# HGRN2 attention with a bilinear feed-forward: the first two units get output tiles, a queue and state sums of their own

## The chip, the core and the metric

The kernel runs on one core of a Trainium2 chip. The metric is the device time of one execution in microseconds (us). The kernel before took 626.97 us (median of 3 runs, 625.71 to 627.32). The engines of the core are TensorE (PE, with its weight load PEld), VectorE (DVE), ScalarE (ACT), GpSimd (POOL) and SyncE (SP). Each works through its own list of instructions in order, and they wait for each other by semaphores.

## The reference, cut to what matters

The first half is a gated linear attention, the second a feed-forward block without an activation function. The output of the first is the input of the second.

```python
# q, k, v, f_logit: (4, 8, 768, 48) = batch, heads, sequence, head_dim
f = 1.0 / (1.0 + np.exp(-f_logit))
for t in range(S):
    state = f[:, :, t, :, None] * state + np.einsum('bhd,bhe->bhde', k[:, :, t], v[:, :, t])
    y[:, :, t] = np.einsum('bhd,bhde->bhe', q[:, :, t], state)

# x: (3072, 384) = the y of all heads side by side; w_a, w_b: (384, 1536); w_out: (1536, 384)
out = (x @ w_a) * (x @ w_b) @ w_out
```

The three weights arrive as 64-bit floats and are turned into 32-bit ones on the chip.

## The kernel before

The attention is cut into 16 units. A unit is one batch, one half of the sequence (384 tokens) and four heads. The feed-forward of a block of 384 tokens needs two units (`NQ` is 2), so the first block can start when units 0 and 1 have delivered their y. The names of the stages:

- `front(u)`: sigmoid of the gates (ACT), running products by scans (DVE), q and k multiplied with them (DVE).
- `scores(u)`: k times q in blocks of 64 tokens (PE), then a causal mask (DVE).
- `turn(u)`: k transposed on PE, copied to `kT` by ACT.
- `within(u)`: v times the masked scores (PE, into `ps_y` or two banks of `ps_f`).
- `gains(u)`: what each sub-block of 64 tokens adds to the state (PE, into `ps_x`), then the states at the sub-blocks' borders, summed one after the other on DVE:

```python
        for n in range(2):
            for c in range(NC):
                for p in range(2):
                    ...
                    for h in range(2):
                        r = slice(SUB * p, SUB * p + SUB)
                        nc.tensor.matmul(
                            ps_x[R * h:R * h + D, p, (n * NC + c) * D:(n * NC + c) * D + D],
                            lhsT=kT[r, n, c, R * h:R * h + D],
                            rhs=t["v"][r, n, c, h * D:h * D + D],
                            start=True,
                            stop=True,
                        )
        ...
        for j in range(NJ - 1 if last else NJ):
            c, p = divmod(j, 2)
            new = ps_x[:, p, 0:2 * NC * D].rearrange("r (n c d) -> r n c d", n=2, c=NC)[:, :, c]
            if before is None:
                nc.vector.tensor_copy(st[:, j], new)
            else:
                nc.vector.tensor_tensor(st[:, j], before, new, ALU.add)
            before = st[:, j]
        before = live[u]["st"][-1]
        if not last:

            for n in range(2):
                end = products_of_f[u][:, n, BLK - 1:BLK]
                nc.vector.tensor_scalar(before[:, n], before[:, n], end, math.exp(-MIDDLE), ALU.mult, ALU.mult)
```

- `across(u)`: the states times q (PE, added to what `within` left), then y copied out of PSUM and sent by DMA into `xT`, the input of the feed-forward with channels on partitions:

```python
        y = sb1.tile([128, 2 * NC, 2, SUB], FP32, tag="y", name="y")

        whole = [(0, 0, 0, 128)] if ps[0] is y_banks[0] else [(0, 0, 0, D), (0, R, R, D)]
        for p, e, r, rows in (*whole, (1, R, 0, D), (1, 0, R, D)):
            copy = nc.vector.tensor_copy if u in FIRST and p else nc.scalar.copy
            copy(y[r:r + rows, :, p], ps[p][e:e + rows, 0:BLK].rearrange("r (o m) -> r o m", m=SUB))
        give_back(ps)
        ...
        for n in range(2):
            for h in range(2):
                ...
                    queue = nc.scalar if u < NQ and (n + h) % 2 else nc.sync
                    queue.dma_start(out=xT[blk][p:p + w, kt], in_=y[row:row + w, n])
```

The pool `sb1` has one buffer for each tag, so all units share one y tile. Each unit sends its y in five transfers.

- `load_weights()` starts the load of one piece of the weights (SP). `begin(n)` and `end(n)` turn piece n into 32-bit floats: four ACT instructions and one of POOL in `begin`, two of DVE in `end`. Piece 0 and 1 are the first 128 columns of w_b and w_a, pieces 2 and 3 the next 256 columns of each.
- `up(blk, ft)`: one 128-column tile of `x @ w_b` and of `x @ w_a` on PE, 384 tokens wide, three `kt` steps each; `product()` multiplies the two.

The order in which all this is issued is written out by hand for the beginning. In the kernel before, from unit 0's last steps to the first feed-forward tile:

```python
        within(0)
        gains(0)
        load_unit(NSET, "f")
        load_weights()
        next(fronts[2])
        turn(1, True)
        across(0)
        load_weights()
        scores(1, True)
        end(2)
        within(1, True)
        load_unit(2, "q")
        gains(1)
        across(1)
        load_weights()
        next(fronts[2])
        next(fronts[3])
        end(3)
        next(fronts[2])
        up(0, 0)
```

After this beginning a loop issues the rest: the feed-forward with the remaining attention units in between.

Of the kernel before, what the change touches and what calls it, by code (L numbers as in the profile page):

```python
# [25 lines left out]
R = 64  # L26
# [52 lines left out]
def by_quotients(ctx, tc, q, k, f_logit, v, moe_w_a, moe_w_b, moe_w_out, out, ident, weights, bad):  # L79
# [171 lines left out]
    def halves(x):  # L251
        return x.rearrange("p n s -> p (n s)")

    def front(u):

        t = sets[u % NSET]
        x = halves(t["f"])
        F = halves(products_of_f[u])
        inv = invs[u % 2 if u < 2 * NQ else 0]
        if u in FIRST:  # L260
            nc.scalar.activation(F, x, AF.Sigmoid)
        nc.scalar.activation(inv, x, AF.Sigmoid, bias=less, scale=-1.0, accum_out=tails[:, u:u + 1])  # L262
        if u not in FIRST:
            nc.scalar.activation(x, x, AF.Sigmoid)

        nc.gpsimd.tensor_scalar(inv, inv, EXP_K, 1.0, ALU.mult, ALU.add)  # L266
        yield
        none = zero.broadcast_to((128, BLK))
        for n in range(2):
            c = slice(n * BLK, n * BLK + BLK)  # L270
            nc.vector.tensor_tensor_scan(F[:, c], F[:, c], none, math.exp(MIDDLE), ALU.mult, ALU.add)
        nc.vector.tensor_tensor(held[:, u], products_of_f[u][:, :, BLK - 1], least, ALU.is_ge)
        yield

        start = sb2.tile([128, 2, NC - 1], FP32, tag="start", name="start")
        nc.vector.reciprocal(start, products_of_f[u].rearrange("p n (c m) -> p n c m", m=C)[:, :, 0:NC - 1, C - 1])
        for n in range(2):
            for c in range(NC):
                w = slice(n * BLK + c * C, n * BLK + c * C + C)
                first = start[:, n, c - 1:c] if c else math.exp(-MIDDLE)  # L280
                nc.vector.tensor_tensor_scan(inv[:, w], inv[:, w], none[:, 0:C], first, ALU.mult, ALU.add)
        yield
        nc.vector.tensor_tensor(halves(t["q"]), halves(t["q"]), F, ALU.mult)
        nc.vector.tensor_tensor(halves(t["k"]), halves(t["k"]), inv, ALU.mult)
        live[u] = {}
        yield
# [68 lines left out]
    def gains(u):  # L355

        _, half, _ = unit(u)
        t, kT = sets[u % NSET], live[u]["kT"]
        last = half == NH - 1
        for n in range(2):  # L360
            for c in range(NC):
                for p in range(2):
                    if last and c == NC - 1 and p == 1:
                        continue
                    for h in range(2):
                        r = slice(SUB * p, SUB * p + SUB)
                        nc.tensor.matmul(  # L367
                            ps_x[R * h:R * h + D, p, (n * NC + c) * D:(n * NC + c) * D + D],
                            lhsT=kT[r, n, c, R * h:R * h + D],
                            rhs=t["v"][r, n, c, h * D:h * D + D],  # L370
                            start=True,
                            stop=True,
                        )
        st = sb3.tile([128, NJ, 2, D], FP32, tag="st", name="st")
        before = live[u - NQ]["st"][NJ] if half else None
        live[u]["st"] = [before] + [st[:, j] for j in range(NJ - 1 if last else NJ)]
        for j in range(NJ - 1 if last else NJ):
            c, p = divmod(j, 2)
            new = ps_x[:, p, 0:2 * NC * D].rearrange("r (n c d) -> r n c d", n=2, c=NC)[:, :, c]
            if before is None:  # L380
                nc.vector.tensor_copy(st[:, j], new)
            else:
                nc.vector.tensor_tensor(st[:, j], before, new, ALU.add)
            before = st[:, j]
        before = live[u]["st"][-1]
        if not last:

            for n in range(2):
                end = products_of_f[u][:, n, BLK - 1:BLK]
                nc.vector.tensor_scalar(before[:, n], before[:, n], end, math.exp(-MIDDLE), ALU.mult, ALU.mult)  # L390
# [19 lines left out]
    def across(u):  # L410

        b, half, qd = unit(u)
        qf, st, ps = halves(sets[u % NSET]["q"]), live[u]["st"], live[u]["y"]

        for n, c, o in reversed(list(each())) if half else each():
            for p in range(2):
                j = 2 * c + p
                if j == half == 0:
                    continue
                for h in range(2):  # L420
                    r, e = slice(R * h, R * h + D), R * (p ^ h)
                    nc.tensor.matmul(  # L422
                        ps[p][e:e + D, o:o + SUB],
                        lhsT=st[j][r, n],
                        rhs=qf[r, tokens(n, c, p)],
                        start=False,
                        stop=True,
                        skip_group_check=True,
                    )
        y = sb1.tile([128, 2 * NC, 2, SUB], FP32, tag="y", name="y")  # L430

        whole = [(0, 0, 0, 128)] if ps[0] is y_banks[0] else [(0, 0, 0, D), (0, R, R, D)]
        for p, e, r, rows in (*whole, (1, R, 0, D), (1, 0, R, D)):
            copy = nc.vector.tensor_copy if u in FIRST and p else nc.scalar.copy
            copy(y[r:r + rows, :, p], ps[p][e:e + rows, 0:BLK].rearrange("r (o m) -> r o m", m=SUB))  # L435
        give_back(ps)
        y = y.rearrange("r (n c) p m -> r n (c p m)", n=2)

        blk = b * NH + half
        if qd == 0:  # L440
            xT[blk] = sb2.tile([128, NKT, BLK], FP32, tag="xT", name="xT")
        for n in range(2):
            for h in range(2):
                ch, row, left = (4 * qd + 2 * n + h) * D, R * h, D
                while left:
                    kt, p = divmod(ch, 128)
                    w = min(left, 128 - p)

                    queue = nc.scalar if u < NQ and (n + h) % 2 else nc.sync
                    queue.dma_start(out=xT[blk][p:p + w, kt], in_=y[row:row + w, n])  # L450
                    ch, row, left = ch + w, row + w, left - w
        live.pop(u - NQ, None)
        if u >= NQ:
            load_unit(u + NSET)
# [246 lines left out]
    with tc.manual_schedule():  # L701
# [11 lines left out]

        load_unit(0, "f")
        load_unit(1, "f")
        next(fronts[0])
        load_unit(1, "q")
        load_unit(0, "q")
        load_unit(1, "k")
        load_weights()  # L720
        load_unit(0, "k")
        load_weights()
        patterns()
        next(fronts[0])
        load_weights()
        next(fronts[0])
        load_unit(1, "v")
        next(fronts[1])
        next(fronts[1])
        next(fronts[0])  # L730
        load_unit(0, "v")
        next(fronts[1])
        begin(3)
        load_unit(2, "k")
        load_unit(2, "f")
        scores(0)
        load_unit(2, "v")
        next(fronts[1])
        turn(0, True)
        within(0)  # L740
        gains(0)
        load_unit(NSET, "f")
        load_weights()
        next(fronts[2])
        turn(1, True)
        across(0)
        load_weights()
        scores(1, True)
        end(2)
        within(1, True)  # L750
        load_unit(2, "q")
        gains(1)
        across(1)
        load_weights()
        next(fronts[2])
        next(fronts[3])
        end(3)
        next(fronts[2])


        up(0, 0)
        next(fronts[2])
        load_unit(NSET, "q")
        begin(4.5)
        load_weights()
        product()
        load_unit(NSET, "v")
        end(4)
        scores(2, True)
        up(0, 1)  # L770
        next(fronts[3])
        load_unit(NSET + 1, "q")
        end(5)
        load_unit(NSET, "k")
        end(6)
        within(2)
        load_unit(NSET + 1, "f")
        load_unit(NSET + 1, "k")
        turn(2, True)
        load_weights()  # L780
        gains(2)
        load_unit(NSET + 1, "v")
        next(fronts[3])
        next(fronts[3])
        product()
        begin(7)
        up(0, 2)
        product()
        across(2)
        up(0, 3)  # L790
        begin(8)
        scores(3)
        turn(3, True)
        within(3)
        gains(3)
        across(3)
        up(0, 4)
        end(7)
        product()
        product()  # L800
        end(8)

# [446 lines left out]
```

## Time and profile before

| what | before |
| --- | --- |
| time, median of 3 runs | 626.97 us |
| span of the profiled execution | 624.1 us |
| PE busy | 588.6 us (94%) |
| DVE busy | 377.8 us (61%) |
| ACT busy | 221.6 us (36%) |
| POOL busy | 63.0 us (10%) |
| PE's share of the chain that ended last | 89% |

The busy times are sums over the whole span. What matters for one stage is read from that stage: the table by windows gives, for a stretch of time, the busy time of each engine, the clock that was granted to TensorE (1.00 is full speed) and the share of the 16 DMA engines that was busy. The view of waits says which instruction's end ended an idle time. The chain follows the last instruction back to whatever released it. In these views L435 is the copy of y out of PSUM, L450 the transfer of y into xT, L469 the feed-forward's matmuls in `up`, L216 the last step of the weights' conversion, L367 the matmuls of `gains`, L381 and L383 the states on DVE, and L188 the load of a piece of the weights. fp32 matmuls appear twice in the counts: `gains` has 24 matmuls and x48 in the trace, `up` 6 and x12. "ACTq" and "SPq" are the queues' own instructions, such as issuing a transfer.

### The profile page before, as it was taken

To read this page: it belongs to the slowest core of one execution; us is meant where nothing else is said; L and a number is where in the kernel's file an instruction comes from. 1 tells how busy PE (TensorE), PEld (TensorE's weight loads), DVE (VectorE), ACT (ScalarE), POOL (GpSimd) and SP (SyncE) were. 2 spreads that over 40 slices of the span, in tenths; PEclk is the share of its full clock that TensorE was granted. 3 is DMA by queue.
4 is the path that set the end of the run, shared out by engine and by line. 5 is a ranking of instruction groups with operands and counts; after the bars stand their busy time and mean duration, and the time that the engine had idled before them with its cause. 6 is when DMAs were issued, how large, how long until landed. Compare 5 with 4: busy or idle time off the path is not lost.

```text
span 624.1 us, 13969 instructions
## 1 busy us (share of the span) xinstructions
PE 588.6 (94%) x5922; PEld 534.5 (86%) x5922; DVE 377.8 (61%) x748; ACT 221.6 (36%) x400; POOL 63.0 (10%) x58
## 2 busy tenths in 40 slices
PE   0759899999999999999999999999999999999995
PEld 0626555558998999999999999999999999999995
DVE  6777445797877567746676476756665244534541
ACT  5578499822332243224312332233311232022200
POOL 6334154410000000000000000000000000000000
PEclk9969999999999999999999999999999999999998
DMA  8886875000045404040404003050001000000000
GB/s 215 230 274 188 181 254 193 1 1 1 32 121 114 100 2 96 6 118 1 97 1 120 28 14 85 1 122 2 21 0 46 26 8 13 2 27 0 1 26 30
DMA packets 30343, 43.65 MB, mean 70 GB/s; under 512 B 3776, under 2 KB 24896, under 8 KB 30272
## 3 DMA queue, kind: packets, MB, share of 16 engines
q1 hardware_dynamic: 29984, 42.38, 25.2%
q8 instruction: 48, 0.79, 0.6%
q10 hardware_dynamic: 288, 0.30, 0.2%
q14 instruction: 23, 0.19, 0.1%
HBM read 33.23 MB, written 4.72 MB: 61 GB/s over the span
## 4 chain that ended last, share of the span: by engine, by line
PE 89%; DMA 4%; ACT 2%; DVE 2%; SPq 1%; issue 0%; ACTq 0%; DVEq 0%
PE ps_f L542 42%; PE ps_f L610 25%; PE ps_f L469 14%; DMA xT<-y 2%; PE ps_x L319 2%; PE ps_y L401 2%; PE ps_x L367 2%; PE ps_y L422 1%; PE ps_x L347 1%; DMA raw<-in_moe_w_b_dram 1%; DMA q_in<-in_q_dram 1%; SPq L154 1%; DVE h L605 0%; SPq L150 0%; ACTq L450 0%
## 5 line engine op out<-in xcount | busy, mean ns | idle before, releaser
L542 PE MATMUL ps_f<-xT,w_ba 128*128 128x192 f32 x864 | 155.7, 327 | 0.0
L547 DVE TENSOR_TENSOR groups<-ps_f,groups 128x384 f32<-128x384 f32 x144 | 80.1, 557 | 117.6 <-ACT groups L559 102.5
L542 PEld LDWEIGHTS ps_f<-xT,w_ba 128*128 128x128 f32 x864 | 142.3, 190 | 0.6
L469 PE MATMUL ps_f<-xT,w_ba 128*128 128x384 f32 x288 | 97.3, 497 | 7.5 <-DVE w_ba L216 6.0
L469 PEld LDWEIGHTS ps_f<-xT,w_ba 128*128 128x128 f32 x288 | 54.9, 193 | 47.1 <-DVE w_ba L216 7.1
L542 PE MATMUL ps_f<-b_sb,raw 128*128 128x192 f32 x432 | 82.2, 326 | 0.0
L542 PEld LDWEIGHTS ps_f<-b_sb,raw 128*128 128x128 f32 x432 | 72.2, 190 | 0.2 <-ACT groups L550 0.2
L610 PE MATMUL ps_f<-w_out,h 128*128 128x192 f32 x288 | 51.8, 330 | 0.0
L550 ACT COPY groups<-ps_f 128x384 f32<-128x384 f32 x36 | 17.2, 479 | 94.9 <-PE ps_f L542 94.8
L610 PE MATMUL ps_f<-w_out,groups 128*128 128x192 f32 x288 | 50.9, 327 | 0.0
L610 PE MATMUL ps_f<-spare,h 128*128 128x192 f32 x288 | 49.4, 327 | 0.2 <-DVE h L605 0.2
L610 PEld LDWEIGHTS ps_f<-w_out,groups 128*128 128x128 f32 x288 | 47.4, 190 | 0.1
L610 PEld LDWEIGHTS ps_f<-w_out,h 128*128 128x128 f32 x288 | 46.8, 190 | 0.6
L610 PEld LDWEIGHTS ps_f<-spare,h 128*128 128x128 f32 x288 | 46.8, 190 | 0.7 <-issue 0.5
L205 POOL TENSOR_SCALAR h<-h 128x768 f32<-128x768 f32 (+1 forms) x20 | 40.7, 2035 | 49.9 <-ACT h L202 49.9
L266 POOL TENSOR_SCALAR inv<-inv 128x768 f32<-128x768 f32 x14 | 13.5, 962 | 303.8 <-ACT inv L262 301.6
L572 DVE TENSOR_TENSOR groups<-groups 128x384 f32<-128x384 f32 x72 | 36.6, 550 | 0.0
L605 DVE TENSOR_TENSOR o<-ps_f,u 128x192 f32<-128x192 f32 x36 | 12.9, 357 | 39.1 <-PE ps_f L610 38.9
L559 ACT COPY groups<-ps_f 128x384 f32<-128x384 f32 x36 | 17.2, 479 | 53.0 <-PE ps_f L542 53.0
L435 ACT COPY y<-ps_y 48x384 f32<-48x384 f32 (+1 forms) x43 | 20.5, 476 | 25.9 <-PE ps_y L422 21.5
L542 PE MATMUL ps_f<-xT,raw 128*128 128x192 f32 x144 | 29.4, 327 | 0.0
L542 PE MATMUL ps_f<-b_sb,w_ba 128*128 128x192 f32 x144 | 29.3, 326 | 0.0
(113 smaller groups left out, 691.3 us busy)
## 6 DMA issues: line engine op xcount, KB each, us to landing
q_in<-in_q_dram SPq DMA_DIRECT2D x32, 144.0 KB, 4.5
k_in<-in_k_dram SPq DMA_DIRECT2D x32, 144.0 KB, 3.6
v_in<-in_v_dram SPq DMA_DIRECT2D x16, 288.0 KB, 5.1
raw<-in_moe_w_out_dram SPq DMA_DIRECT2D x6, 768.0 KB, 4.4
out_dram<-o SPq DMA_DIRECT2D x24, 192.0 KB, 1.9
f_in<-in_f_logit_dram SPq DMA_DIRECT2D x28, 144.0 KB, 3.0
xT<-y SPq DMA_DIRECT2D x46, 72.0 KB, 2.2
raw<-in_moe_w_b_dram SPq DMA_DIRECT2D x4, 768.0 KB, 7.3
```

The source lines that it names most:

```text
L205: nc.gpsimd.tensor_scalar(h, h, HI_MAX, None, ALU.min)
L266: nc.gpsimd.tensor_scalar(inv, inv, EXP_K, 1.0, ALU.mult, ALU.add)
L319: nc.tensor.matmul(ps[h][SUB * p:SUB * p + SUB, o:o + SUB], lhsT=kf[r, tokens(n, c, p)], rhs=qf[r, tokens(n, c, p)], start=True, stop=True,)
L435: copy(y[r:r + rows, :, p], ps[p][e:e + rows, 0:BLK].rearrange("r (o m) -> r o m", m=SUB))
L469: nc.tensor.matmul(ps[nm][:, 0:BLK], lhsT=w[:, kt, ft * 128:ft * 128 + 128], rhs=x[:, kt], start=kt == 0, stop=kt == NKT - 1,)
L542: nc.tensor.matmul(to[:, g], lhsT=w[:, g, j], rhs=x, start=start and g == 0, stop=True, skip_group_check=True)
L547: nc.vector.tensor_tensor(c[:, :, k, i], x, y, ALU.add)
L550: nc.scalar.copy(p1, x0)
L559: nc.scalar.copy(u3, x0)
L572: nc.vector.tensor_tensor(to[:, :, 2 * j + k], a[:, :, k], b[:, :, k], ALU.mult)
L605: nc.vector.tensor_tensor(to, x, y, op)
L610: nc.tensor.matmul(to, lhsT=x[:, i], rhs=w[:, i], start=first and i == 0, stop=i == HFT - 1, skip_group_check=True)
```

## The change

For units 0 and 1 (`FIRST`) four things change, and the order of the beginning changes with them.

1. Each of the two has a y tile of its own, in a part of the tile `groups` that is used later. All its transfers into xT go out from ScalarE's queue; unit 0's y is copied by ACT alone, unit 1's by ACT and DVE.
2. The states come from running sums that PE forms in PSUM: the matmul of sub-block pair c is repeated over all pairs up to c and accumulated, 48 matmuls in place of 24. Then ACT copies the odd sums, and three wider DVE instructions make all states in place of six narrow ones.
3. The product that carries the last state into the other half of the sequence, and the check `held` of the gates, move from `gains` and `front` into `carry(u)`, which is issued later, behind y.
4. The order of loads, weights' conversions and stages in the beginning.

What it is for: y of unit 1 need not wait until unit 0's y has been sent, SP's queue holds no transfers of y that keep later loads waiting, and the chain of small DVE instructions ahead of `across` is shorter.

```diff
         for n in range(2):
             c = slice(n * BLK, n * BLK + BLK)
             nc.vector.tensor_tensor_scan(F[:, c], F[:, c], none, math.exp(MIDDLE), ALU.mult, ALU.add)
-        nc.vector.tensor_tensor(held[:, u], products_of_f[u][:, :, BLK - 1], least, ALU.is_ge)
+        if u not in FIRST:
+            check(u)
...
+        at_once = u in FIRST
...
-                        nc.tensor.matmul(
-                            ps_x[R * h:R * h + D, p, (n * NC + c) * D:(n * NC + c) * D + D],
-                            lhsT=kT[r, n, c, R * h:R * h + D],
-                            rhs=t["v"][r, n, c, h * D:h * D + D],
-                            start=True,
-                            stop=True,
-                        )
+                        for ci in range(0 if at_once else c, c + 1):
+                            nc.tensor.matmul(
+                                ps_x[R * h:R * h + D, p, (n * NC + c) * D:(n * NC + c) * D + D],
+                                lhsT=kT[r, n, ci, R * h:R * h + D],
+                                rhs=t["v"][r, n, ci, h * D:h * D + D],
+                                start=ci == 0 or not at_once,
+                                stop=ci == c,
+                            )
...
+        if at_once:
+            sums = [ps_x[:, p, 0:2 * NC * D].rearrange("r (n c d) -> r c n d", n=2, c=NC) for p in range(2)]
+            even, odd = (st.rearrange("r (c p) n d -> r p c n d", p=2)[:, p] for p in range(2))
+            nc.scalar.copy(odd, sums[1])
+            nc.vector.tensor_copy(even[:, 0], sums[0][:, 0])
+            nc.vector.tensor_tensor(even[:, 1:], sums[0][:, 1:], odd[:, 0:NC - 1], ALU.add)
+            nc.vector.tensor_tensor(odd, sums[0], odd, ALU.add)
+            return
...
-        y = sb1.tile([128, 2 * NC, 2, SUB], FP32, tag="y", name="y")
+        if u in FIRST:
+            y = groups[:, NTG, u * 2 * BLK:u * 2 * BLK + 2 * BLK].rearrange("r (o p m) -> r o p m", p=2, m=SUB)
+        else:
+            y = sb1.tile([128, 2 * NC, 2, SUB], FP32, tag="y", name="y")
...
-            copy = nc.vector.tensor_copy if u in FIRST and p else nc.scalar.copy
+            copy = nc.vector.tensor_copy if u == 1 and p else nc.scalar.copy
...
-                    queue = nc.scalar if u < NQ and (n + h) % 2 else nc.sync
+                    queue = nc.scalar if u in FIRST else nc.sync
```

The loads at the very start, in the order of SP's queue: before f0 f1 q1 q0 k1 w_b(0) k0 w_a(0) w_b(1) v1 v0 k2 f2 v2; after f0 f1 w_b(0) w_a(0) q0 w_b(1) f2 k0 v0 q1 v1 k1 v2 w_a(1) (the number is the unit, or for weights the piece of that matrix). The same stretch as above, after:

```python
        within(0)
        gains(0)
        next(fronts[2])
        load_unit(2, "v")
        scores(1, True)
        load_weights()
        turn(1, True)
        load_unit(2, "k")
        load_unit(NSET, "f")
        load_unit(NSET + 1, "k")
        end(3)
        load_unit(2, "q")
        across(0)
        next(fronts[2])
        within(1, True)
        gains(1)
        end(4)
        across(1)
        begin(4.5)
        next(fronts[2])
        next(fronts[3])
        next(fronts[2])
        load_unit(NSET, "q")
        up(0, 0)
        ...
        next(fronts[3])
        carry(0)
        scores(2, True)
        up(0, 1)
```

The order from unit 2 to the end of the beginning changes too: `turn(2)` now stands ahead of `within(2)`, `carry(1)` between `turn(3)` and `within(3)`, and some loads and conversions are shifted. The loop behind it is unchanged.

## The prediction

> **What bounds the kernel now.** The page first. PE is busy for 94% of the span and holds 89% of the chain. The rows of the 40 slices (15.6 us each) show where it is not:
>
> ```profile
> PE   0759899999999999999999999999999999999995
> ...
> PEclk9969999999999999999999999999999999999998
> ```
>
> Only the first five slices have room, some 80 us; behind them PE is full whatever the beginning does. The kernel can gain or lose only by when PE gets its feed-forward work. The table by windows narrows that (columns: length, then busy us of PE, PEld, DVE, ACT, POOL with counts, granted clock, DMA share, GB/s):
>
> ```profile
> 31.87:37.87 6.00, 0.01 (x2) 0.01 (x1) 4.56 (x9) 2.47 (x5) 0.45 (x1) 0.61 0.60 123
> 37.87:40.50 2.63, 1.65 (x3) 0.53 (x3) 2.63 (x6) 2.63 (x4) 2.04 (x2) 0.50 1.05 396
> 40.50:44.76 4.26, 4.26 (x12) 2.24 (x16) 2.39 (x4) 4.17 (x7) 3.10 (x2) 0.66 1.06 342
> 44.76:72.99 28.23, 25.95 (x432) 16.74 (x433) 19.49 (x40) 18.12 (x27) 7.25 (x5) 1.00 0.71 187
> ```
>
> PE stands still from 31.87 to 37.87, its clock falls to half, and the first feed-forward tile ends at 44.76. From there to 72.99, where it passes to the next block, PE idles 28.23 - 25.95 = 2.3 us. So 44.76 is the time that the change must beat. The chain between says why it is so late (start, length, what):
>
> ```profile
> 24.57 0.49 ACT y L435
> ...
> 27.68 5.38 DMA xT<-y
> ...
> 33.17 0.56 DVE y L435
> 33.77 0.56 DVE y L435
> ...
> 34.40 0.53 ACTq L450
> 34.96 0.62 ACTq L450
> 35.60 4.76 DMA xT<-y
> 40.36 0.14 issue
> 40.50 4.26 PE ps_f L469 x8
> ```
>
> Unit 0's y is sent; its last transfer lands at 33.05; only then is unit 1's y copied, into the same tile. Unit 1's last transfer leaves at 35.60 and lands at 40.36. The view of waits for 20 to 40 us puts a size on it:
>
> ```profile
> ACT y L435 <- DMA xT<-y: 8.1, 1, 8.1
> ...
> PE ps_f L469 <- DVE w_ba L216: 6.0, 1, 6.0
> ...
> DVE y L435 <- DMA xT<-y: 2.1, 1, 2.1
> ```
>
> `across(1)` ends at 31.04, so the shared tile costs 2.1 us, DVE's wait, not the 8.1 us for which ACT had nothing to do. PE's second matmul (37.87) was released by a conversion that ended at 37.81, behind the same copies in DVE's order; but PE still needed y until 40.36.
>
> **What the Trainium skill says.** "DMA: Bandwidth & Descriptors", section "Issuing engines are not separate DMA queues": transfers started by different engines share the same 16 DMA engines and interleave, and a second issuer saves only sequencer time, usually small beside the transfer. The trace agrees on the sharing: y's small last transfers took 5.4 and 4.8 us beside weight loads, 1.8 to 3.0 us otherwise. Sequencer time is not small here: three issues held ACT from 26.31 to 28.37 and from 34.40 to 36.21, 0.6 us each. "TensorE: Matmul & The Clock Gate", section "What's actually happening": PE falls to half clock after an idle window of about 3.4 us and needs about as long of work to recover. The trace agrees roughly: 0.50 from 34, full speed at some 42.6, 4.7 us after PE restarts. "VectorE: DVE Perf Modes", section "The TRN2 errata — SBUF-src ops pay a fixed extra latency per instruction": its table gives every VectorE instruction a fixed part beside its length, from PSUM too, so few wide ones are cheaper. The trace agrees: 96 elements took 0.26 us, 768 took 0.93.
>
> **The change part by part.** I carry the new order forward by hand with durations of the old trace; each engine takes its list in order.
>
> *Start.* k0 moves behind 1.57 MB of weights and f2. Landings in the trace, from issue plus time to landing: f1 6.7; then 0.65 us for half a q, k or f; 1.65 and 1.1 for the small weight pieces; 2.0 for a large one; about 1 for v. In the new order: w_b(0) 8.1, w_a(0) 9.5, q0 10.8, w_b(1) 12.8, f2 14.1, k0 15.4. Before, k0 landed at 13.85 and its multiplication ran 14.14 to 15.40. Both scans of F now stand together and two checks (0.53 and 0.16) leave, but DVE must wait for k0 anyway: 15.4 to 16.4. `scores(0)` starts at 16.5, not 15.6: **0.9 us lost**. Then unit 1's reciprocal and six scans (2.5, as at 15.32 to 17.83) and the mask (0.93): 19.9; `within(0)` to 21.1. v0 no longer holds it (0.6 us before).
>
> *Sums on PE.* 48 matmuls, x96. x48 took 1.21 us here and 0.71 us later, so 1.9: to 23.0 (before 22.32). States: ACT's copy of 288 elements 0.4, then DVE on 96, 192 and 288 elements, estimated from the rows above at 0.26 + 0.36 + 0.46: 24.5. Before they were done at 24.1: six instructions took 1.7 us, now four in series take 1.5, and PE cannot start `across` after the first. Then `scores(1)` 0.95 and `turn(1)` 1.1 go ahead of `across(0)` 1.0: y0 is complete in PSUM at 26.1 (before 24.55).
>
> *ACT's list*, which I expect to set the end. From 23.4: unit 2's sigmoids 0.94 + 0.19 + 0.85 = 25.4; kT(1) 0.83: 26.2; three copies of y0, 1.45: 27.7; five issues at 0.62, 3.1: 30.8; unit 1's odd sums 0.4: 31.2; conversion of w_a(1), four instructions less overlap 3.7: 34.9; its copies of y1, 0.97: 35.9. DVE beside it: masks to 25.6, conversions of three pieces 0.9 + 0.9 + 1.5, scans of f2 1.8 and check 0.16: 31.0; states of unit 1 from 31.2 to 32.3; second half of w_a(1) only after ACT's 34.9, 0.96: 35.9; two copies of y1, 1.14: 37.0. `across(1)` is over by 33.5, so y1 does not wait for PE.
>
> *Sending y1.* First issue 36.5, five at 0.62: the last begins at 39.0. No weights are being issued then (SP waits at f4, for POOL), so 2.3 us as undisturbed: **lands 41.3**, against 40.36. The tile's wait is gone, and ACT's queue has taken its place. What is removed: 2.1 us of waiting and about 2.4 us of disturbance in the last transfer. What is added: 0.9 at the start, 1.0 by the new order to y0, 1.2 for two more issues in series, and 2.7 for a conversion and its DVE half between `across(1)` and the copies.
>
> *PE.* Idle stays near 6 us ahead of the restart, now 39.3, so the clock returns near 44.0 instead of 42.6: 0.25 us more at half speed. First tile done 1.2 us later than 44.76.
>
> *After it*, the same matmuls. `turn(2)` ahead of `within(2)` hides a 0.24 us wait for kT; the 1.2 us wait of `across(3)` for DVE stays; DVE and the weights come early enough; I credit 0.4 in all. Beyond 73 us nothing moves. Sum: +0.9 + 0.25 - 0.4 = +0.75, so **627.7 us**.
>
> **The rivals.** (a) *The gain as meant.* If ACT's list is not late, y1 is copied at 31.1 when `across(1)` ends as before, issues run to 34.8 and y lands near 36.6: PE starts 3.7 us earlier, and since it is full behind that, the time becomes about 623. For it: both waits named above are removed, and SP stops waiting for y (its loads stood still 5.3 and 4.4 us). Against it: the order of ACT's list. (b) *The new wait is longer.* Four conversions' halves and five issues share ACT; y1's last two issues also wait for transfers of w_b(2) and q2 on the same semaphores. If those land after 39, or k0 lands at 17, add 2 to 3 us: 630. (c) *Hidden.* The early loads and conversions take out most of the 2.3 us of idle between 44.76 and 72.99 and pay for the late start: 626 to 627.
>
> **Range and chances.** My steps in series are some fifteen with about 0.3 us error each, 1.2 us together; rival (a) in part would take 3 us off, (b) add 3. So 624.0 to 631.0. 2% is 12.5 us: PE's whole idle time in the first 73 us, less what loading forces, is hardly more, and no rival reaches it. Faster by over 2% 0.01, within 2% 0.98, slower 0.01. Within that I hold a slightly slower kernel for a little likelier than a faster one.
>
> **What would show it.** Right: `scores(0)` begins near 16.5; ACT's wait for xT at L435 is gone; ACT issues y0 until about 30.8 and copies y1 only near 35, behind the conversion's L202 to L209; y1's transfers land in about 2.3 us, the last near 41.3; half clock still around 34 to 44; the stretch from first tile to next block near 28 us; all gaps equal behind 75 us. Wrong: y1 copied before 33 (rival a); last landing after 43 or a semaphore wait inside the five issues (b); first tile late but PE back level by 75 us (c); or a difference that arises in the 550 us behind the beginning, which no step of mine allows.

## The result and the profile after

The changed kernel takes 636.66 us (median of 4, 635.17 to 638.92), the kernel before, timed beside it, 626.75 us (median of 4, 625.71 to 627.32): ratio 1.0163, 95% interval 1.0128 to 1.0198. It is 9.9 us slower; the prediction was 627.7 us, in 624.0 to 631.0.

The profiled execution of the changed kernel is the slowest of its four (638.92 us, span 637.1), so its differences add up to 13.0 us, not 9.9. Its page, rows of PE and of PE's clock in 40 slices (15.9 us each):

```profile
PE   0739789999999999999999999999999999999996
...
PEclk9869979999999999999999999999999999999999
```

PE's third slice falls from 5 to 3 tenths, as foreseen in kind. New is a second dip: PE's fifth and sixth slices are 7 and 8 (8 and 9 before), and its clock's sixth is 7 (9 before). The windows of the changed kernel (columns as in the table before: length, busy us of PE, PEld, DVE, ACT, POOL, clock, DMA share, GB/s):

```profile
39.61:45.77 6.16, 0.00 (x0) 0.03 (x1) 5.83 (x12) 2.05 (x3) 0.68 (x1) 0.50 0.65 187
45.77:51.51 5.74, 5.74 (x14) 2.94 (x16) 0.00 (x0) 4.65 (x8) 3.31 (x3) 0.60 0.22 58
51.51:81.91 30.40, 24.85 (x432) 16.23 (x431) 19.66 (x44) 16.73 (x26) 6.76 (x3) 0.99 0.70 193
...
81.91:86.91 5.00, 5.00 (x8) 2.83 (x9) 0.00 (x0) 2.07 (x3) 0.71 (x1) 0.50 1.02 223
```

And of the kernel before, from the start of its second block:

```profile
72.99:77.99 5.00, 5.00 (x16) 3.01 (x17) 0.88 (x2) 4.04 (x6) 2.13 (x1) 1.00 1.04 246
```

The first tile ends at 51.51 instead of 44.76: 6.75 us. From there to the second block it takes 30.40 instead of 28.23: 2.17 us, with 30.40 - 24.85 = 5.6 us of idle instead of 2.3. And the second block begins at half clock: 8 matmuls in 5 us, where the kernel before did 16. Behind the restart the span has 637.1 - 81.91 = 555.2 us left, before 624.1 - 72.99 = 551.1: 4.1 us.

The first loss is read from ACT's timeline in the changed kernel (start, length, what; in brackets the idle time before it and what ended that):

```profile
29.86 1.47 ACT L460 COPY groups<-ps_y 128x384 f32<-128x384 f32 x3 [1.01 <-PE ps_y L443]
30.86 4.26 ACTq L475 DMA_DIRECT2D xT<-groups  x5
35.21 0.40 ACT L388 COPY st<-ps_x 128x288 f32<-128x288 f32 x1 [3.89 <-issue]
35.51 0.89 ACT L202 ACTIVATE h<-raw 128x768 f32<-128x768 f32 x1
...
38.12 1.07 ACT L209 ACTIVATE spare<-spare 128x768 uint16<-128x768 bf16 x1
39.05 0.95 ACT L460 COPY groups<-ps_f 48x384 f32<-48x384 f32 x2
40.97 3.09 ACTq L475 DMA_DIRECT2D xT<-groups  x5
```

The reader sees the list that the prediction named, in its order, each part about 4 us later than it said (3.8 to 4.5). While ACT issues y0, the gains of unit 1 lie ready in PSUM from 32.17 on, and PE waits for the copy of the odd sums: 3.79 us for L389, which waits for L388. The chain of the changed kernel around 74 us shows the second loss (start, length, what):

```profile
74.23 7.39 DMA xT<-y
81.62 0.29 issue
81.91 2.26 PE ps_f L494 x3
```

y of unit 3 lands 7.39 us after its first transfer is issued; PE waits 4.02 us for it and restarts at half clock. SyncE's queue just before (start, length, what), the same kernel:

```profile
64.41 3.83 SPq L475 DMA_DIRECT2D xT<-y  x5
68.34 1.01 SPq L154 DMA_DIRECT2D f_in<-in_f_logit_dram  x2
...
71.30 0.42 SPq L156 DMA_DIRECT2D v_in<-in_v_dram  x1
71.78 0.46 SPq L188 DMA_DIRECT2D raw<-in_moe_w_a_dram  x1
72.28 1.55 SPq L154 DMA_DIRECT2D q_in<-in_q_dram  x2
74.23 3.56 SPq L475 DMA_DIRECT2D xT<-y  x5
```

The four loads of a later unit behind y2 (f, k, q and v) stand there in the kernel before too; the large piece w_a(4) (L188) and q of unit 4 behind it are new in this place.

### The profile page after: what moved, and what is told of

Read it like the earlier page. It is cut to its first block, busy times and chain, and to the rows that moved or that the text cites. A ratio compares the mean times of both kernels' runs of the same rounds, so it can differ in the third digit from the quotient of the medians.

```text
span 637.1 us, 14154 instructions
## 1 busy us (share of the span) xinstructions
PE 594.1 (93%) x6018; PEld 539.2 (85%) x6018; DVE 374.8 (59%) x740; ACT 223.5 (35%) x404; POOL 62.7 (10%) x58
## 4 chain that ended last, share of the span: by engine, by line
PE 87%; issue 4%; DVE 3%; DMA 2%; ACT 1%; POOL 1%; SPq 0%; DVEq 0%; POOLq 0%; ACTq 0%
PE ps_f L567 41%; PE ps_f L635 24%; PE ps_f L494 15%; PE ps_y L422 2%; PE ps_x L324 2%; PE ps_y L443 1%; PE ps_x L374 1%; DMA xT<-y 1%; POOL h L205 1%; PE ps_x L352 1%; DMA xT<-groups 1%; DMA f_in<-in_f_logit_dram 1%; DVE h L630 0%; ACT kT L356 0%; DVE inv L286 0%
## 5 line engine op out<-in xcount | busy, mean ns | idle before, releaser
L494 PE MATMUL ps_f<-xT,w_ba 128*128 128x384 f32 x288 | 100.7, 512 | 10.2 <-DMA xT<-groups 6.2
L324 PE MATMUL ps_x<-q_in,k_in 48*64 48x64 f32 x672 | 13.7, 226 | 18.3 <-DMA q_in<-in_q_dram 17.6
L511 DVE TENSOR_TENSOR groups<-ps_f,b_sb 128x384 f32<-128x384 f32 x24 | 13.2, 553 | 29.4 <-ACT spare L207 9.7
```

Source lines behind the costliest of these rows:

```text
L324: nc.tensor.matmul(ps[h][SUB * p:SUB * p + SUB, o:o + SUB], lhsT=kf[r, tokens(n, c, p)], rhs=qf[r, tokens(n, c, p)], start=True, stop=True,)
L494: nc.tensor.matmul(ps[nm][:, 0:BLK], lhsT=w[:, kt, ft * 128:ft * 128 + 128], rhs=x[:, kt], start=kt == 0, stop=kt == NKT - 1,)
L511: nc.vector.tensor_tensor(products(blk)[:, :, ft], a, b, ALU.mult)
```

## The experiments

Theory A: the new order costs the time, by what it puts ahead of y0, y1 and y3 in each engine's list. Rival B: the new code for units 0 and 1 costs it (y on one queue, sums on PE, the carry's new place), and the order only shifts it. Kernels are told by their code (before or changed) and order (old or new). Each is timed beside the kernel before, whose median was 626.6 to 627.1 each time. In the table "first tile" is the end of the first feed-forward tile, "restart" the start of the second block, "y3" PE's wait there and "rest" the span behind the restart; these four are from the profiled execution, in us. That is one execution, up to 2.3 us away from its kernel's median (the changed kernel 2.3 above, e1 2.0 under, e3 1.2 above), so differences of 1 to 2 us between two rows are not shown by it alone.

| kernel | median | first tile | restart | y3 | rest |
| --- | --- | --- | --- | --- | --- |
| before | 626.75 | 44.76 | 72.99 | 0.52 | 551.1 |
| changed | 636.66 | 51.51 | 81.91 | 4.02 | 555.2 |
| e5, new code, old order | 631.98 | 50.79 | 79.85 | 1.00 | 551.0 |
| e6, old code, new order | 634.16 | 49.09 | 78.25 | 2.79 | 554.2 |
| e3, own tiles only | 625.75 | 45.81 | 74.15 | 0.55 | 551.1 |
| e7, e3 + one queue | 627.84 | 46.38 | 75.11 | 1.00 | 551.0 |
| e12, e3 + sums on PE | 628.67 | 48.07 | 76.31 | 0.52 | 550.9 |
| e11, e3 + carry late | 626.16 | 44.26 | 73.05 | 0.60 | 551.1 |
| e8, e3 + sums + carry | 628.80 | 48.18 | 76.86 | 0.56 | 550.7 |
| e1, changed, y3 ahead of loads | 637.46 | 50.83 | 78.51 | 0.66 | 555.2 |
| e2, changed, y1 ahead of conversion | 636.90 | 51.63 | 82.79 | 3.43 | 552.3 |
| e4, changed, old first loads | 636.39 | 50.15 | 80.00 | 3.47 | 553.7 |
| e9, changed, f4 later | 637.02 | 50.48 | 80.40 | 3.35 | 554.0 |
| e10, e2 + e4 + e9 + two queues | 636.83 | 50.02 | 80.72 | 2.37 | 554.1 |
| e13, e9 + loads ahead of y2 | 632.82 | 52.81 | 80.31 | 0.48 | 551.9 |
| e14, e13's loads, e3's code | 630.31 | 48.79 | 76.33 | 0.53 | 552.1 |
| e15, e14 + old first loads | 628.17 | 47.29 | 74.84 | 0.54 | 551.8 |

The last two columns go together: where y3 is waited for 2.3 us or more, the rest is 552.3 to 555.2; where it is not, 550.7 to 552.1, but for e1. The price is not proportional: e2 waited 3.43 us and kept its full clock behind that.

### Code against order: e5 and e6

```diff
 (e5: changed code; the whole beginning in the old order)
+        carry(0)
         scores(2, True)
...
+        carry(1)
         within(3)
```

> The changed kernel's code (own tiles, ACT's queue alone, sums on PE, carry behind y) in the order of the kernel before; carry(0) ahead of scores(2), carry(1) ahead of within(3). Theory A (the new order makes the loss: late loads at the start, SP's list held by f3 and f4, conversions ahead of y1): most of the 10 us goes, time 626 to 630. Theory B (the code makes it: five issues and the odd sums on ACT in series): most stays, time 633 to 637.

Measured: 631.98 us, ratio 1.0076 (1.0050 to 1.0103).

```diff
 (e6: code of the kernel before; the whole beginning in the new order, without the two calls)
-        carry(0)
         scores(2, True)
...
-        carry(1)
         within(3)
```

> The kernel before's code (shared y tile, two queues, sums on DVE, carry in gains) in the new order. Theory A (order): time 633 to 638, first tile near 50 or later. Theory B (code): time 626 to 629. If both parts of the cross cost little alone, the loss is their combination: ACT's list becomes too long only when the order puts conversions and issues in front of y1.

Measured: 634.16 us, ratio 1.0125 (1.0108 to 1.0142). Code alone costs about 5 us, order alone about 7.5, both 9.9, so each theory holds a part. The late y3 goes with the order: 2.79 us in e6, 1.00 in e5.

### The code's parts in the old order: e3, e7, e8, e11, e12

```diff
 (e3: kernel before with y in own tiles, nothing else)
-        y = sb1.tile([128, 2 * NC, 2, SUB], FP32, tag="y", name="y")
+        if u in FIRST:
+            y = groups[:, NTG, u * 2 * BLK:u * 2 * BLK + 2 * BLK].rearrange("r (o p m) -> r o p m", p=2, m=SUB)
+        else:
+            y = sb1.tile([128, 2 * NC, 2, SUB], FP32, tag="y", name="y")
```

> The kernel before with one thing changed: units 0 and 1 have y tiles of their own; queues, sums and order as before. Theory (the wait for the shared tile is a real cost of 2.1 us and the rest of the change destroys the gain): y1 is copied at 31 to 32 instead of 33.2 to 34.3, the first tile ends 1.5 to 3 us earlier than 44.76 and the time is 623.5 to 625.5. Rival (its transfers then run beside w_b(2) and q2, which end at 35, and the conversion of w_b(1) on DVE stays late): first tile unchanged, time 626 to 627.

Measured: 625.75 us, ratio 0.9981 (0.9973 to 0.9990). This is the only kernel of the study whose interval lies under that of the kernel before, and so it beats both; by 1.2 us, by the ratio. Its profiled execution (626.99 us) doesn't show where: its first tile is even later. What the tile removes, the wait of y1's copy, is gone: ACT and DVE copy y1 as soon as `across(1)` is over, but y1's transfers then run beside weight loads and PE still gets y1 at 40.90.

```diff
 (e7: e3 and ACT's queue)
-                    queue = nc.scalar if u < NQ and (n + h) % 2 else nc.sync
+                    queue = nc.scalar if u in FIRST else nc.sync
...
-            copy = nc.vector.tensor_copy if u in FIRST and p else nc.scalar.copy
+            copy = nc.vector.tensor_copy if u == 1 and p else nc.scalar.copy
```

> The kernel before with own y tiles and all of y's transfers of units 0 and 1 on ACT's queue (unit 0's y copied by ACT alone), nothing else. Theory A: ACT is held 3 us longer by issues but SP is freed, so time 625 to 627.5. Theory B (ACT's issues are the cost): first tile 2 us or more later than with two queues, time 628 to 630.

Measured: 627.84 us, ratio 1.0012 (1.0004 to 1.0020): one queue costs 2.1 us over e3. In the profiled executions 0.9 us of this can be seen: y1 was in its tile 1.6 us earlier in e7 than in e3, but landed only 0.7 us earlier (40.0 against 40.8), and two of PE's twelve matmuls of the first tile that e3 did at 38.01, ahead of y1, were still to be done in e7, so the tile ends 0.6 us later. That the late landing makes the rest of the 2.1 us is likely and not shown. The DMA issues of e7 between 33 and 41 us (transfers of y, number, size, median us to landing):

```profile
xT<-groups ACTq DMA_DIRECT2D x2, 72.0 KB, 6.5
xT<-groups ACTq DMA_DIRECT2D x1, 48.0 KB, 7.0
xT<-groups ACTq DMA_DIRECT2D x1, 24.0 KB, 7.1
```

And of e3, where SyncE issues two of the five itself:

```profile
xT<-groups SPq DMA_DIRECT2D x2, 72.0 KB, 2.4
xT<-groups ACTq DMA_DIRECT2D x1, 72.0 KB, 5.0
xT<-groups ACTq DMA_DIRECT2D x1, 48.0 KB, 2.1
xT<-groups ACTq DMA_DIRECT2D x1, 24.0 KB, 2.0
```

In e3 SyncE issues its part of y1 first, and w_a(2) and w_b(3) behind it at 35.41 and 36.04; in e7 it is relieved of y and issues both at 31.25 and 31.91, ahead of y1. The DMA engines were busy for a share of 0.19 in e3 from y1's first issue to 36 us, and 0.96 in e7.

```diff
 (e8: changed code, old order as e5, with the two queues of the kernel before)
-            copy = nc.vector.tensor_copy if u == 1 and p else nc.scalar.copy
+            copy = nc.vector.tensor_copy if u in FIRST and p else nc.scalar.copy
...
-                    queue = nc.scalar if u in FIRST else nc.sync
+                    queue = nc.scalar if u < NQ and (n + h) % 2 else nc.sync
```

> As the run of the new code in the old order, but y of units 0 and 1 goes out by SP's and ACT's queue as before, with unit 0's y copied by ACT and DVE. So it holds own tiles, sums on PE and the carry behind y. Theory A: 625 to 627, the sums on PE neither gain nor lose more than 1 us. Theory B: if the odd sums on ACT and the doubled matmuls are what costs, 629 or more.

Measured: 628.80 us, ratio 1.0032 (1.0020 to 1.0045), 3.1 us over e3 and 3.2 under e5, which differs from it by the one queue alone. The next two runs divide the 3.1.

```diff
 (e11: e3 with the check and the carry behind y)
+        if not at_once:
+            carry(u)
...
+        carry(0)
         scores(2, True)
...
+        carry(1)
         within(3)
```

> The kernel before with y in tiles of its own and with the carry and the check of the first two units behind y, but with VectorE's own sums and the old order and queues. If the carry on the path was worth its roughly 0.3 us (two small VectorE instructions a unit): 625.3 to 625.8, a little under the 625.75 of tiles alone. If the 3.2 us of the pair (sums on PE and carry) come from the carry's new place, ahead of scores(2)'s work on VectorE: 628 to 629.

Measured: 626.16 us, ratio 0.9994 (0.9983 to 1.0004). No gain over e3, and no loss that the intervals separate.

```diff
 (e12: e8 with the carry left in gains)
             nc.vector.tensor_tensor(odd, sums[0], odd, ALU.add)
+            carry(u)
             return
...
-        carry(0)
...
-        carry(1)
```

> The kernel before with y in tiles of its own and sums formed on PE, the carry left where it was, old order and queues. If the sums' 96 instead of 64 or so matmuls at half clock and the copy on ScalarE between them cost the 3.2 us: 628.5 to 629.5. If the carry does: 625.5 to 626.5.

Measured: 628.67 us, ratio 1.0031 (1.0019 to 1.0042), 2.9 us over e3. The sums on PE cost it; the carry's new place costs nothing that these runs separate. Unit 1's states in e12, from its timeline:

```profile
30.13 2.70 PE L374 MATMUL ps_x<-v_in,kT 64*48 64x48 f32 x94
32.87 0.40 ACT L388 COPY st<-ps_x 128x288 f32<-128x288 f32 x1 [5.73 <-PE ps_x L374]
33.30 0.26 DVE L389 COPY st<-ps_x 128x96 f32<-128x96 f32 x1 [2.21 <-ACT st L388]
...
33.62 0.45 PE L444 MATMUL ps_f<-q_in,st 48*48 48x64 f32 x4 [0.78 <-DVE st L389]
33.86 0.46 DVE L391 TENSOR_TENSOR st<-ps_x,st 128x288 f32<-128x288 f32 x1
```

And in e3, with VectorE's sums:

```profile
29.43 1.20 PE L367 MATMUL ps_x<-v_in,kT 64*48 64x48 f32 x46
30.69 0.26 DVE L381 COPY st<-ps_x 128x96 f32<-128x96 f32 x1 [0.87 <-PE ps_x L367]
30.98 1.40 DVE L383 TENSOR_TENSOR st<-st,ps_x 128x96 f32<-128x96 f32 x5
31.00 2.24 PE L422 MATMUL ps_f<-q_in,st 48*48 48x64 f32 x40 [0.37 <-DVE st L381]
```

From the first gains that stand together to the start of `across(1)`: 3.5 us in e12, 1.6 in e3. Unit 0 loses in the same way, from its gains to `across(0)` with `turn(1)` between them 3.75 us against 2.61, and 1.9 and 1.1 make the 2.9 that was measured. The doubled matmuls take 1.5 us more; what they were to shorten, DVE's chain of 1.7 us, lay beside `across` for all but its first 0.26 us. The Trainium skill's "VectorE: DVE Perf Modes" (section "The TRN2 errata — SBUF-src ops pay a fixed extra latency per instruction"), cited in the prediction for the fixed part of each instruction, is borne out here too: 288 elements in 0.46 us against 1.40 for five of 96; but this was no time on the path.

### Single parts of the order undone in the changed kernel: e1, e2, e4, e9, e10

```diff
 (e1)
         turn(3, True)
-        load_weights()
         carry(1)
         within(3)
-        load_unit(NSET + 1, "q")
         gains(3)
         across(3)
+        load_weights()
+        load_unit(NSET + 1, "q")
```

> The changed kernel with two loads moved: the fifth piece of w_a and unit 4's q go out behind unit 3's y instead of ahead of it. Theory (loads ahead of y3 in SP's queue make y3 late): y3's last transfer lands about 3 us after its issue instead of 7.4, PE's 4.0 us wait ahead of the second block falls below 1 us, the half clock behind that wait goes too (about 3 us), and the time becomes 629.5 to 631.5. Rival (y3 is late only because everything before it is late): the wait stays near 4 us and the time near 636.

Measured: 637.46 us, ratio 1.0181 (1.0158 to 1.0205). y3 landed 2.0 us after its last issue and the restart came 3.4 us earlier; then w_a(4) landed only at 86.84, and PE waited 1.81 us near 91 for a copy that stood behind its conversion in ACT's list, and 1.24 us near 93 for the conversion's last step. The wait had moved.

```diff
 (e2)
         gains(1)
-        end(4)
         across(1)
+        end(4)
```

> The changed kernel with the conversion of w_a(1) moved behind across(1), so that ACT and DVE copy y1 first. Theory (ACT's list is what makes y1 late): y1 is copied near 37 instead of 39 to 41.5, its last transfer lands 3 to 4 us earlier (near 42), the first tile ends near 48 instead of 51.5 and the time falls by 3 to 4 us to about 633. Rival (the transfers or the conversion itself set the first tile, which needs w_a(1)'s conversion by its dependences): first tile within 1 us of 51.5, time near 636.

Measured: 636.90 us, ratio 1.0167 (1.0135 to 1.0199). y1 was no longer copied behind a conversion, yet it still landed near 45.8: in this execution the beginning ran 2.3 us later (`scores(0)` at 19.94; in the seven kernels with the new first loads it began between 16.87 and 19.94, in those with the old ones between 15.30 and 16.12), and ACT stood 3.56 us in y1's five issues. No gain in the time, and what was before y1 is now behind it: `scores(2)` waits 1.29 us for the conversion.

```diff
 (e4)
         patterns()
+        load_unit(0, "q")
+        next(fronts[0])
+        load_unit(0, "k")
         load_weights()
         load_weights()
-        next(fronts[0])
-        load_unit(0, "q")
-        load_weights()
         next(fronts[1])
         next(fronts[0])
+        load_unit(0, "v")
+        load_weights()
-        load_unit(2, "f")
-        load_unit(0, "k")
         next(fronts[1])
-        load_unit(0, "v")
+        load_unit(2, "f")
```

> The changed kernel with q0, k0 and v0 loaded ahead of the weights and of f2. Theory (k0's late landing at 16.4 starts the chain late): k0 lands near 11, scores(0) starts near 14.5 instead of 17.6, and 1 to 3 us of it reach the end: 634 to 635.5. Rival (q1 and k1, v1 or PE's own issuing set unit 1's start): scores(0) earlier, but first tile within 1 us of 51.5 and time near 636.5.

Measured: 636.39 us, ratio 1.0170 (1.0145 to 1.0195). `scores(0)` began at 15.38 instead of 17.60, and of these 2.2 us the first tile got 1.4 and the time 0.3, which is within the noise (four runs of each, 635.4 to 639.4 and 635.2 to 638.9). PE reached the middle of `scores(1)` 1.8 us earlier and stood there 2.55 us (1.57 in the changed kernel), so it went on only 0.8 us earlier (25.35 instead of 26.12); y3 was late as before.

```diff
 (e9)
         product()
-        load_unit(NSET + 1, "f")
         load_unit(NSET, "v")
...
         load_weights()
+        load_unit(NSET + 1, "f")
```

> The changed kernel with one load moved: f of unit 4 is issued behind w_a(4) instead of ahead of v of unit 3, so that SyncE's list no longer stands at it from 39.9 to 49.25 us for GpSimd's memset. Theory A (the whole list of loads behind this one is late, and y3's landing and the second cold clock follow from it): w_b(3), w_a(3) and w_b(4) go out about 9 us earlier, w_a(4) and q4 before 65 us, y3 lands about 2 us after its issue, the wait of 4.0 us and the half clock at 82 to 90 us are gone; restart of the second block at 75 to 77, time 629 to 632. Rival B (the loads only collide earlier, with y1): y1's landing passes 46 us, first tile as late or later, time 636 or more. Rival C (the order is late by its compute alone): no change, 636 to 637.

Measured: 637.02 us, ratio 1.0171 (1.0149 to 1.0192). v3, w_b(3) and w_a(3) went out at 40.9 to 42.3 instead of 50.1 to 51.1, so SyncE no longer stood still at f4; but w_a(4) and q4 stand behind y2 in SyncE's order whatever happens earlier, and went out at 70.6 and 71.1, still ahead of y3. Theory A as I had put it for this run falls: the hold at f4 is not the root.

```diff
 (e10: e4's, e2's and e9's edits, and)
-            copy = nc.vector.tensor_copy if u == 1 and p else nc.scalar.copy
+            copy = nc.vector.tensor_copy if u in FIRST and p else nc.scalar.copy
...
-                    queue = nc.scalar if u in FIRST else nc.sync
+                    queue = nc.scalar if u < NQ and (n + h) % 2 else nc.sync
```

> The changed kernel with four parts of its order or queue undone together: q0, k0 and v0 loaded ahead of the weights, the conversions of end(4) behind y1, f of unit 4 issued behind w_a(4), and y on two queues. If the order's cost of about 7 us is the sum of these (scores(0) 2 us later, y1 behind a conversion about 1 to 2, SyncE held at f4 about 4, queue 2): 627 to 630. If each alone only moves the wait (as the load order and the conversion did alone), and together too: 633 to 637.

Measured: 636.83 us, ratio 1.0162 (1.0145 to 1.0179). Four undone parts, no gain: `scores(0)` began at 15.38, but PE stood 3.35 us in the middle of `scores(1)`, the first tile is 1.5 us earlier, and y3 is still waited for 2.37 us.

### The loads between y2 and y3, then the rest: e13, e14, e15

```diff
 (e13: e9, and)
-        load_weights()
+        load_weights(2)
+        load_unit(NSET + 1, "q")
         load_unit(NSET + 1, "f")
...
         turn(3, True)
-        load_weights()
         carry(1)
         within(3)
-        load_unit(NSET + 1, "q")
```

> The changed kernel with three loads moved: w_a(4) and q of unit 4 ahead of y2's transfers instead of between y2's and y3's, and f of unit 4 behind them. Theory A (the second loss, between the first tile and the second block, is these loads in front of y3): y3 lands some 2.2 us after its last issue, PE waits under 0.7 us for it and keeps its full clock, restart of the second block 28.2 us after the first tile's end as before; with a first tile at 50 to 51.5 that gives a restart at 78.5 to 79.5, span 551 more, time 630 to 632. Rival B (the wait moves to something else, as it did when these two loads went behind y3): 636 to 637.

Measured: 632.82 us, ratio 1.0099 (1.0066 to 1.0132): 3.8 us of the 9.9 come back, and 4.2 against e9 (637.02, 1.0149 to 1.0192), from which e13 differs by these two calls alone. The chain of e13 around y3:

```profile
77.99 2.18 DMA xT<-y
...
80.31 3.79 PE ps_f L494 x11
```

y3's last transfer lands in 2.18 us, the wait is 0.48, and the second block starts at full clock: 16 and 17 matmuls in its first two stretches of 5 us, as in the kernel before; the changed kernel did 8 and 15. First tile to restart takes 27.5 us, 0.7 less than before the change. This although its first tile is the latest of all (52.81): w_b(3) to w_b(4), no longer held at f4, now run beside y1's transfers, which land at about 47.3.

```diff
 (e14: code of e3, in the order of e13)
-        carry(0)
         scores(2, True)
...
-        carry(1)
         within(3)
```

> The new order alone (own code of the kernel before but for y in tiles of its own: VectorE's sums, carry where it was, two queues), with the same three loads moved. The order with the old code took 634.16. If own tiles are worth 1.2 here and the loads 3 to 5 us: 628.5 to 630. What it stays above 625.75 is then what the new order costs in the first tile alone. If the loads matter only together with the slower code: 633.

Measured: 630.31 us, ratio 1.0064 (1.0047 to 1.0081). Leaving out one queue, the sums on PE and the late carry gives 2.5 us here (the intervals of e13 and e14 still touch); first tile 4.0 us earlier in the profiles.

```diff
 (e15: e14 with e4's edit)
```

> As the run before, and q0, k0 and v0 are loaded ahead of the weights as in the old order: scores(0) at 15.4 instead of 17 to 18.6. If the start's 2 to 3 us go through to the first tile: 626 to 627.5, near the kernel before. If the first tile is set by y1's landing behind conversions and not by the start: within 0.5 us of the run before.

Measured: 628.17 us, ratio 1.0022 (1.0013 to 1.0031). The old first loads give 2.1 us (`scores(0)` at 15.63 instead of 17.66, first tile 1.5 us earlier); in e4 the same edit gave 0.3, with y3's wait and the longer stop of PE behind it. What stays, 2.4 us over e3, belongs to the rest of the new order and wasn't taken apart.

So the 9.9 us are, from the changed kernel down to the one before, in medians: 3.8 loads ahead of y3; 2.5 code; 2.1 late k0; 2.4 the rest of the order; less 1.0 (626.75 - 625.75) that own tiles gain. The steps depend on their order, and each is known to 1 or 2 us: the code costs 6.2 us by e5 against e3 in the old order (3.2 the one queue, 2.9 the sums on PE, 0.1 the carry).

## Why the prediction was wrong

**Right.** The bound: the first tile decides, and PE is full behind it. The tile's wait went and ACT's list took its place, in the order foretold: y0's issues, unit 1's odd sums, the conversion L202 to L209, y1's copies. SyncE stood at f4 for GpSimd from 39.94 to 49.25 us. The clock fell to half. Rival (b), the new wait longer, was the nearest; it was given 630. Its sign came (y1's last landing behind 43), its cause only in part: k0 landed late as it feared, but the five issues of y1 held no wait for a semaphore, 0.52 to 0.60 us each.

**Failed step 1, "After it, the same matmuls ... I credit 0.4 in all. Beyond 73 us nothing moves."** This is the largest single error. The step looked at matmuls and not at SyncE's list: w_a(4) and q4 had moved in front of y3's transfers. Because y3 took 7.39 us to land, PE waited 4.02 us and restarted at half clock: +2.17 in the stretch and +4.1 behind it in the profiled execution, where -0.4 was predicted; e13 gets 3.8 us of median back by moving these loads with f4, and 4.2 over e9, where f4 alone was moved; then the stretch is 0.7 us shorter than before, so the credit of 0.4 was of the right kind. In the changed kernel the two calls stand between `turn(3)` and `gains(3)`, in plain sight.

**Failed step 2, "Sums on PE".** The matmuls were sized rightly (1.9 us forecast, about 2.2 measured at 21.99). The comparison "six instructions took 1.7 us, now four in series take 1.5" was wrong in kind: of the six all but the first were hidden under `across`, the four are not. The sentence even says that PE "cannot start `across` after the first", and gives it no price. e12 against e3 gives the price: 2.9 us.

**Failed step 3, "ACT's list" in its times.** y0 was in PSUM at 29.86, not 26.1. Of the 3.8 us, 1.1 come from k0 (`scores(0)` at 17.60, said 16.5), 1.57 from a stop of PE in the middle of `scores(1)` that no term of the prediction allowed for (see the last section), and the rest from `turn(1)` and `across(0)` (1.54 and about 1.6 us; 1.1 and 1.0 forecast). Then five issues took 4.26 us and not 3.1, so the copy of unit 1's sums ended at 35.61, not 31.2, and that of y1 began at 39.05, not 34.9.

**Failed step 4, "No weights are being issued then ..., so 2.3 us as undisturbed".** SyncE indeed issued nothing, but what it had issued until 39.9 (q2, w_a(2) and q3, issued from 36.22 to 39.94) was still under way: the DMA share between 39.61 and 45.77 is 0.65, and the five took 2.7 to 4.5 us. y1 landed at 45.5, said 41.3.

**Start.** k0's multiplication began at 16.43, said 15.4: 2.0 us lost at `scores(0)`, not 0.9; by e15 these 2 us count in full (2.1 us) once y3 is no longer late. The credit for one queue (rival (a), SyncE no longer waiting for y) was a cost: 2.1 us in e7, 3.2 in e5 against e8. The Trainium skill's "DMA: Bandwidth & Descriptors" (section "Issuing engines are not separate DMA queues"), cited in the prediction, holds in this: the issuing engines share the same 16 DMA engines. Taking y off SyncE let its loads go out ahead of y1, and the DMA engines were busy for 0.96 of the time in e7, 0.19 in e3.

**Readings.** Three points of the prediction do not come out of the profile before; its sum does not rest on them. The clock was back at 43.4, not 42.6 (0.50 until then), 5.5 us after PE's restart at 37.87. Of the two waits of SyncE's loads for y, "5.3 and 4.4 us", the 5.3 belongs to a later unit; for units 0 and 1 they are 3.2 and 4.4. And what is removed (4.5) and added (5.8) for y1 differs by 1.3, where its own landing times differ by 0.9.

The range failed because its errors were taken as independent, "some fifteen with about 0.3 us error each". What was mis-sized ahead of y1 lies in one series, all of it with the same sign, and the late y3, the largest error, was no term of the range at all.

## What to carry to other kernels

In a beginning where each engine takes its list in order, price a reordering by going through every engine's list up to the last transfer that PE waits for, the loading queue's too: here two loads in front of a small transfer cost 3.8 to 4.2 us, by the wait and by the clock behind it. A chain of small instructions that feeds matmuls one by one is not on the path except for its first; exchanging it for fewer wide ones behind more matmuls must pay for the overlap that is lost. And several late things can hide each other: undoing one showed nothing here beyond the noise of about 2 us (e1, e2, e4, e9), and undoing four together that left y3 late showed nothing either (e10), so undo from the kernel that has the fewest left, or remove the latest wait first.

## What the runs showed of the hardware

- Five issues of y on ACT, 24 to 72 KB each, held it from 3.09 to 4.26 us, and ACT did no other work meanwhile. Most single issues took 0.5 to 0.64 us; in the 4.26 us one of the five took 1.64 us.
- In the profiles of the changed kernel, e1, e2, e4, e9, e10 and e13, which have the same matmuls in the same order up to there, PE stops behind the same matmul of `scores(1)`, and no view names what it waits for ("issue"). It stood there 0.93 us where it arrived last (e2, at 27.4) and 3.35 where it arrived first (e10, at 22.2). In the DMA view each of these seven has one transfer of 16 KB of instructions (queue q8) 2.4 to 2.6 us before PE goes on: at 23.6 in the changed kernel (PE on at 26.12), 25.8 in e2 (28.30), 23.1 in e10 (25.58). The same distance, 2.5 to 2.7, stands ahead of the stops in e5, e14 and e15. This points to PE waiting for its next instructions; no run tests it. The stop of 1.72 us ahead of `within(1)` in the kernel before is another: it ends 0.1 us after VectorE has made the first half of the mask that `within(1)` reads (from 26.26, 0.55 us).
- After 4.02 us without work PE's clock was 0.50 for the next 5 us and 0.90 in the 5 after; after 0.5 us it was 1.00. Those 4 us of waiting thus cost about 3 us more: some 10 matmuls fewer in 10 us, at 5 us / 16 = 0.31 us each. How long PE idles does not settle it alone: after 3.43 us in e2 the clock stayed at 1.00, after 2.37 us in e10 and 2.79 us in e6 it fell to 0.50, 0.7 to 0.8 us after PE had started again. That differs from the idle window of about 3.4 us that the prediction cites.
